# Squared-ReLU attention and a mixture of adapters: two stages through a transposed copy in DRAM, against one pipeline of 64x64 tiles

## The chip, the cores and the metric

One core of a Trainium2 chip runs the whole kernel as one launch. The metric is the device time of that core in microseconds, the median of repeated executions; lower is better.

## What is computed

For 8 batches of 12 heads, q, k and v are 448 x 64 each, in f32. The attention has no softmax; its output becomes 3584 rows of 768, on which each row picks the best two of eight adapters of rank 16:

```python
scores = scale * np.matmul(q, k.transpose(0, 1, 3, 2))
attn = np.maximum(scores, 0.0) ** 2 / S
attn_out = np.matmul(attn, v)
x = attn_out.transpose(0, 2, 1, 3).reshape(B * S, H * D)
logits = x @ w_gate
topk = np.argpartition(-logits, 2, axis=1)[:, :2]
...
delta[mask] += w[mask, k, None] * ((x[mask] @ A[e]) @ B[e])
return x + delta
```

The weights w are the softmax over the two chosen logits.

## The kernel before

The work has two stages that follow one another.

The attention stage goes over the 8 batches, and in each over 12 heads in two groups of six. `do_prepass` (L74 to L84) loads a group of q and of k as f32 on SP's queue, casts q on ScalarE (L81) and k on VectorE (L83) to bf16 and stores both into DRAM tensors `q_bf` and `k_bf`. `do_transpose` (L86 to L95) reads them back with a transposing DMA, so that `qT` and `kT` have the 64 values of a head on the partitions. v is loaded in four pieces a batch (L104) and cast in one instruction on ScalarE (L111).

For each head there are four chunks of up to 128 keys (128, 128, 128 and 64). A chunk is one score matmul (L125, 64 rows of the array, 128 or 64 columns, 448 queries streamed), one ReLU with scale (two heads of three on ScalarE, L137; every third on VectorE, L135), one square on VectorE (L138), and one value matmul (L139, 128 or 64 rows, 64 columns, 448 streamed) that accumulates `outT` over the chunks. A head's result is copied from PSUM into `xt` (L149 on VectorE, L151 on ScalarE), which holds x transposed for all 3584 rows.

The adapter stage goes over 7 chunks of 512 rows. It computes z (L184, all adapters at once as 128 columns), the logits of 128 rows at a time (L199), the routing weights in eight short instructions on VectorE and an exponential on ScalarE (L207 to L221), expands and transposes them (L226 to L230), multiplies (L233), applies B in f32 (L238), adds x (L245), transposes back in f32 (L250), copies (L256) and stores (L257).

The order of the instructions on each engine comes from the framework's own scheduling of the program; the pools' buffers (six for scores, two for outT) limit how far it runs ahead. The pools of the attention stage are closed before those of the adapter stage are opened.

Of the kernel before, what the change touches and what calls it, by code (L numbers as in the profile page):

```python
# [9 lines left out]
F32 = mybir.dt.float32  # L11
F32R = mybir.dt.float32
BF16 = mybir.dt.bfloat16


@with_exitstack
def kernel(
# [10 lines left out]
    nc = tc.nc  # L28
# [28 lines left out]
    k_bf = k_bf_flat[:TOT].rearrange("(b h s d) -> b h s d", b=B, h=H, s=S)

    TCH = (S + 127) // 128
    tsz = [min(128, S - i * 128) for i in range(TCH)]  # L60

    attn_ctx = ExitStack()
    attn_sbuf = attn_ctx.enter_context(tc.tile_pool(name="attn_sbuf", bufs=4))
    attn_psum = attn_ctx.enter_context(tc.tile_pool(name="attn_psum", bufs=2, space=bass.MemoryType.PSUM))
    vb_pool = attn_ctx.enter_context(tc.tile_pool(name="vb", bufs=2))
    pp_pool = attn_ctx.enter_context(tc.tile_pool(name="pp", bufs=2))

    zt = pp_pool.tile([128, 1], BF16, tag="zt", bufs=1)
    nc.vector.memset(zt, 0.0)
    nc.sync.dma_start(out=q_bf_flat[TOT:].rearrange("(p f) -> p f", p=128), in_=zt)  # L70
    nc.sync.dma_start(out=k_bf_flat[TOT:].rearrange("(p f) -> p f", p=128), in_=zt)

    qT_pool = attn_ctx.enter_context(tc.tile_pool(name="qT_pool", bufs=3))

    def do_prepass(b, g):
        for i, (src, dst) in enumerate(((qflat, qbf2), (kflat, kbf2))):
            tf = pp_pool.tile([128, PPC], F32, tag=f"tf{i}")
            nc.sync.dma_start(out=tf, in_=src[b, g])
            tb = pp_pool.tile([128, PPC], BF16, tag=f"tb{i}")
            if i == 0:  # L80
                nc.scalar.copy(tb, tf)  # L81
            else:
                nc.vector.tensor_copy(tb, tf)  # L83
            nc.sync.dma_start(out=dst[b, g], in_=tb)  # L84

    def do_transpose(b, g):  # L86
        qT = qT_pool.tile([128, HS, S], BF16, tag="qT")
        kT = qT_pool.tile([128, HS, S], BF16, tag="kT")
        q_src = bass.AP(tensor=q_bf.tensor, offset=(b * H + g * HS) * S * Dh,
                        ap=[[Dh, HS * S], [1, 2 * Dh]])  # L90
        k_src = bass.AP(tensor=k_bf.tensor, offset=(b * H + g * HS) * S * Dh,
                        ap=[[Dh, HS * S], [1, 2 * Dh]])
        nc.sync.dma_start(out=qT.rearrange("p h s -> p (h s)"), in_=q_src, transpose=True)  # L93
        nc.sync.dma_start(out=kT.rearrange("p h s -> p (h s)"), in_=k_src, transpose=True)
        return qT, kT  # L95

    bg_list = [(b, g) for b in range(B) for g in range(NSPLIT)]
    do_prepass(0, 0)
    qTkT = {(0, 0): None}
    for b in range(B):  # L100
        v_f = vb_pool.tile([128, TCH, H, Dh], F32, tag="v_f")
        for tc_i in range(TCH):
            ts = tsz[tc_i]
            nc.sync.dma_start(  # L104
                out=v_f[:ts, tc_i],
                in_=v[b, :, tc_i * 128 : tc_i * 128 + ts, :].transpose([1, 0, 2]),
            )
        if tsz[-1] < 128:
            nc.vector.memset(v_f[64:128, TCH - 1], 0.0)
        v_bf = vb_pool.tile([128, TCH, H, Dh], BF16, tag="v_bf")  # L110
        nc.scalar.copy(v_bf, v_f)  # L111

        for h in range(H):
            g = h // HS
            bg_idx = b * NSPLIT + g
            if h % HS == 0:
                if bg_idx + 1 < len(bg_list):
                    do_prepass(*bg_list[bg_idx + 1])
                qT, kT = do_transpose(b, g)
            hg = h - g * HS  # L120
            outT_ps = attn_psum.tile([64, S], F32, tag="outT", bufs=2)
            for tc_i in range(TCH):
                ts = tsz[tc_i]
                scores_ps = attn_psum.tile([128, 512], F32, tag="scores", bufs=6)
                nc.tensor.matmul(  # L125
                    out=scores_ps[:ts, :S],
                    lhsT=kT[:Dh, hg, tc_i * 128 : tc_i * 128 + ts],
                    rhs=qT[:Dh, hg, :],
                    start=True,
                    stop=True,  # L130
                )
# [6 lines left out]
                nc.vector.tensor_mul(attn2_bf[:ts], attn_bf[:ts], attn_bf[:ts])  # L138
                nc.tensor.matmul(  # L139
                    out=outT_ps,  # L140
                    lhsT=v_bf[:ts, tc_i, h, :],
                    rhs=attn2_bf[:ts],
                    start=(tc_i == 0),
                    stop=(tc_i == TCH - 1),
                )
            p0 = (h % 2) * 64
            dst = xt[p0 : p0 + 64, h // 2, b * S : b * S + S]
            if h % 2:
                nc.vector.tensor_copy(dst, outT_ps)  # L149
            else:  # L150
                nc.scalar.copy(dst, outT_ps)  # L151

    attn_ctx.close()

    wg_sb = const_pool.tile([128, DO, E], BF16)
    nc.gpsimd.dma_start(out=wg_sb, in_=moe_w_gate.rearrange("(do di) e -> di do e", di=128))

    A_sb = const_pool.tile([128, DO, E, R], BF16)
    for do in range(DO):
# [128 lines left out]
```

## Time and profile before

| | us |
|---|---|
| median of 3 runs | 541.85 |
| lowest and highest run | 539.98, 545.13 |
| the profiled execution: span from the first to the last instruction | 544.2 |
| TensorE matmul busy | 456.5 |
| VectorE busy | 337.3 |
| ScalarE busy | 199.8 |

The page gives the profiled execution by its span alone. It lies inside the runs. Busy time of TensorE's matmuls counts from a matmul's start to its modelled end, so two that follow closely overlap; the pitch between two starts is read from the timeline. A row of the timeline that merges n instructions gives the start of the first and the time to the end of the last.

### The profile page before, as it was taken

The numbers are of one execution on the slowest core, as the hardware profiler recorded it, in microseconds if no ns is written. First come the engines' busy times: TensorE is split into PE (matmuls) and PEld (weight loads), VectorE is DVE, ScalarE is ACT, GpSimd is POOL, SyncE is SP. The second block draws the span as 40 slices with busy tenths as digits, with TensorE's granted clock in tenths as the row PEclk, the third lists the DMA queues.
The fourth block names the chain that finished last, engine by engine and source line by source line (L and its number), as shares of the span: only waits on it lengthen the run. The fifth ranks groups of instructions, "written<-read, shape, count | busy, mean of one in ns | idle before, by whom it ended". The sixth has DMA issues, their size and how long they took to land.

```text
span 544.2 us, 4703 instructions
## 1 busy us (share of the span) xinstructions
PE 456.5 (84%) x1253; PEld 134.5 (25%) x1258; DVE 337.3 (62%) x921; ACT 199.8 (37%) x385; POOL 6.9 (1%) x13
## 2 busy tenths in 40 slices
PE   0004999999999999999999999999998798888874
PEld 0001222222221221222122222212222345454532
DVE  1003667566676756756665665766557779897863
ACT  1033374355337445535644554454333111111000
POOL 5000000000000000000000000000000000000000
PEclk9999999999999999999999999999999989896877
DMA  9979929907955981991597199046000013131222
GB/s 100 144 254 255 279 98 255 295 8 203 210 197 126 240 242 45 221 272 70 136 235 237 44 226 263 5 118 136 0 1 0 1 47 137 73 151 59 116 117 116
DMA packets 151292, 77.99 MB, mean 143 GB/s; under 512 B 139361, under 2 KB 139361, under 8 KB 151265
## 3 DMA queue, kind: packets, MB, share of 16 engines
q1 hardware_dynamic: 144240, 77.48, 55.9%
q0 software_dynamic: 7024, 0.21, 2.6%
q8 instruction: 10, 0.16, 0.1%
q14 instruction: 18, 0.14, 0.1%
HBM read 33.84 MB, written 22.02 MB: 103 GB/s over the span
## 4 chain that ended last, share of the span: by engine, by line
PE 76%; DVE 13%; DMA 6%; SPq 2%; issue 2%; ACT 0%; ACTq 0%
PE outT_ps L139 33%; PE scores_ps L125 30%; PE d_ps L238 8%; PE tr_ps L250 4%; DMA tf<-in_k_dram 3%; DVE out_nd L256 3%; DVE xt L149 3%; DVE attn_bf L138 3%; PE zT_ps L184 1%; DMA tf<-in_q_dram 1%; DVE sumT_sb L245 1%; SPq L104 1%; DMA kT<-k_bf 1%; SPq L93 1%; DVE wexpT_sb L230 1%
## 5 line engine op out<-in xcount | busy, mean ns | idle before, releaser
L125 PE MATMUL scores_ps<-qT,kT 64*128 64x448 bf16 (+1 forms) x384 | 191.7, 562 | 48.2 <-DMA kT<-k_bf 48.2
L139 PE MATMUL outT_ps<-attn_bf,v_bf 128*64 128x448 bf16 (+1 forms) x384 | 197.1, 577 | 13.7 <-DVE attn_bf L138 12.5
L138 DVE TENSOR_TENSOR attn_bf<-attn_bf 128x448 bf16<-128x448 bf16 (+1 forms) x384 | 132.9, 381 | 53.6 <-PE outT_ps L139 35.7
L137 ACT ACTIVATE attn_bf<-scores_ps 128x448 bf16<-128x448 f32 (+1 forms) x256 | 122.6, 539 | 100.5 <-DVE attn_bf L138 75.3
L125 PEld LDWEIGHTS <-kT 64*128 64x128 bf16 (+1 forms) x384 | 37.7, 112 | 201.2 <-issue 153.0
L149 DVE CAST xt<-outT_ps 64x448 bf16<-64x448 f32 x48 | 29.6, 618 | 82.5 <-PE outT_ps L139 82.5
L139 PEld LDWEIGHTS <-v_bf 128*64 128x64 bf16 (+1 forms) x384 | 44.4, 133 | 140.0 <-issue 125.7
L135 DVE TENSOR_SCALAR attn_bf<-scores_ps 128x448 bf16<-128x448 f32 (+1 forms) x128 | 74.2, 609 | 1.3 <-PE scores_ps L125 1.3
L151 ACT CAST xt<-outT_ps 64x448 bf16<-64x448 f32 x48 | 25.2, 525 | 101.4 <-PE outT_ps L139 101.4
L238 PE MATMUL d_ps<-zpT_sb,B_sb 128*128 128x512 f32 x84 | 50.4, 739 | 1.5 <-DVE zpT_sb L233 1.4
L250 PE MATMUL tr_ps<-ident,sumT_sb 128*128 128x128 f32 x168 | 30.2, 308 | 11.7 <-DVE out_nd L256 9.6
L83 DVE CAST tb<-tf 128x1344 bf16<-128x1344 f32 x16 | 13.6, 849 | 38.4 <-DMA tf<-in_k_dram 38.4
L245 DVE TENSOR_TENSOR sumT_sb<-d_ps,xt 128x512 f32<-128x512 f32 x42 | 28.8, 689 | 13.0 <-PE d_ps L238 12.8
L111 ACT CAST v_bf<-v_f 128x3072 bf16<-128x3072 f32 x8 | 22.0, 2748 | 26.8 <-DMA v_f<-in_v_dram 26.8
L256 DVE COPY out_nd<-tr_ps 128x768 f32<-128x768 f32 x28 | 26.7, 955 | 7.5 <-PE tr_ps L250 6.8
L250 PEld LDWEIGHTS tr_ps<-ident,sumT_sb 128*128 128x128 f32 x168 | 21.7, 155 | 24.1 <-DVE out_nd L256 14.5
L226 ACT COPY w_exp<-w_sb 128x128 f32<-128x128 f32 x28 | 8.3, 296 | 49.9 <-DVE w_sb L221 24.1
L238 PEld LDWEIGHTS d_ps<-zpT_sb,B_sb 128*128 128x128 f32 x84 | 17.7, 235 | 20.8 <-issue 8.4
L81 ACT CAST tb<-tf 128x1344 bf16<-128x1344 f32 x16 | 20.4, 1310 | 3.5 <-DMA tf<-in_q_dram 2.6
L213 ACT ACTIVATE w_sb<-sub 128x8 f32<-128x8 f32 x28 | 5.8, 208 | 38.9 <-DVE sub L211 30.6
L229 PE MATMUL wexp_ps<-ident,w_exp 128*128 128x128 f32 x28 | 9.4, 338 | 5.6 <-ACT w_exp L226 4.9
L184 PE MATMUL zT_ps<-xt,A_sb 128*128 128x512 bf16 x37 | 12.6, 439 | 1.1 <-DVE xt L149 0.8
(26 smaller groups left out, 98.9 us busy)
## 6 DMA issues: line engine op xcount, KB each, us to landing
tf<-in_q_dram SPq DMA_DIRECT2D x16, 672.0 KB, 6.6
tf<-in_k_dram SPq DMA_DIRECT2D x16, 672.0 KB, 7.6
out_dram<-out_nd SPq DMA_DIRECT2D x28, 384.0 KB, 2.3
v_f<-in_v_dram SPq DMA_DIRECT2D x24, 384.0 KB, 5.0
q_bf<-tb SPq DMA_DIRECT2D x16, 336.0 KB, 2.7
k_bf<-tb SPq DMA_DIRECT2D x16, 336.0 KB, 2.9
v_f<-in_v_dram SPq DMA_DIRECT2D x8, 192.0 KB, 5.6
B_sb<-in_moe_B_dram SPq DMA_DIRECT2D x1, 384.0 KB, 7.5
```

The costliest lines, as they stand in the source:

```text
L111: nc.scalar.copy(v_bf, v_f)
L125: nc.tensor.matmul(out=scores_ps[:ts, :S], lhsT=kT[:Dh, hg, tc_i * 128 : tc_i * 128 + ts], rhs=qT[:Dh, hg, :], start=True, stop=True,)
L135: nc.vector.tensor_scalar(attn_bf[:ts], scores_ps[:ts, :S], relu_scale, 0.0, op0=mybir.AluOpType.mult, op1=mybir.AluOpType.max)
L137: nc.scalar.activation(attn_bf[:ts], scores_ps[:ts, :S], mybir.ActivationFunctionType.Relu, scale=relu_scale)
L138: nc.vector.tensor_mul(attn2_bf[:ts], attn_bf[:ts], attn_bf[:ts])
L139: nc.tensor.matmul(out=outT_ps, lhsT=v_bf[:ts, tc_i, h, :], rhs=attn2_bf[:ts], start=(tc_i == 0), stop=(tc_i == TCH - 1),)
L149: nc.vector.tensor_copy(dst, outT_ps)
L151: nc.scalar.copy(dst, outT_ps)
L238: nc.tensor.matmul(out=d_ps[:, :ncur], lhsT=B_sb[:, do * 128 : do * 128 + 128], rhs=zpT_sb[:, :ncur], start=True, stop=True,)
L245: nc.vector.tensor_add(sumT_sb[:, do, :ncur], d_ps[:, :ncur], xt_c[:, do, :])
L250: nc.tensor.transpose(tr_ps[:ns, do * 128 : do * 128 + 128], sumT_sb[:, do, j * 128 : j * 128 + ns], ident,)
L256: nc.vector.tensor_copy(out_nd[:ns], tr_ps[:ns])
```

## The change

The new kernel keeps what is computed and changes how all of it is laid out and ordered. The 448 positions of a head are taken as 64 partitions times 7 (J), so that a position is 7 p + j. Batches are loaded by POOL with a cast from f32 to bf16 in the DMA, six heads on the lower 64 partitions and six on the upper. A quad is four heads: two slots (sl) times two halves (g, or a on the key side). Two jobs of 14 transposes on TensorE per quad make qT and kT. A step is one j of a quad: four score matmuls, one ReLU, one square, and, two steps later (LAG), four value matmuls, each of 64x64 on its own quarter of the array. The adapter work is written as a generator of short pieces, `job_moe`; one piece runs between the score and the value matmuls of those steps of a quad that don't transpose (j of 0, 2, 4, 5, 6). The order is written out by hand (`manual_schedule`).

The core of the diff, where line numbers of the new kernel in the text below (L112 and so on) are those of its file:

```diff
-    const_pool = ctx.enter_context(tc.tile_pool(name="const", bufs=1))
-    q_bf_flat = nc.dram_tensor("q_bf", (TOT + PAD,), BF16)
-    k_bf_flat = nc.dram_tensor("k_bf", (TOT + PAD,), BF16)
...
-    def do_prepass(b, g):
-    def do_transpose(b, g):
...
+    loads = ctx.enter_context(tc.tile_pool(name="loads", bufs=3))
+    apool = ctx.enter_context(tc.tile_pool(name="apool", bufs=4))
+    ps_s = ctx.enter_context(tc.tile_pool(name="ps_s", bufs=2, space=bass.MemoryType.PSUM))
+    ps_o = ctx.enter_context(tc.tile_pool(name="ps_o", bufs=1, space=bass.MemoryType.PSUM))
+    ps_m = ctx.enter_context(tc.tile_pool(name="ps_m", bufs=2, space=bass.MemoryType.PSUM))
+    ctx.enter_context(tc.manual_schedule())
...
+    def load_batch(b, per_quad=False):
...
+        parts = [(2 * c, 2 * c + 2) for c in range(NC_)] if per_quad else [(0, HH)]
+        for s0, s1 in parts:
+            for t, src in zip(tiles, (qv, kv, vv)):
+                for g in range(2):
+                    nc.gpsimd.dma_start(
+                        out=t[g * PH : g * PH + PH, s0:s1, :], in_=src[b, g, :, s0:s1, :]
+                    )
...
+    def job_transpose(qi, which):
...
+        for j in range(J):
+            for sl in range(2):
+                nc.tensor.transpose(
+                    ps[sl * PH : sl * PH + PH, j * 128 : j * 128 + 128],
+                    src[:, 2 * c + sl, j * Dh : j * Dh + Dh],
+                    identb,
+                )
+        yield
...
+        nc.vector.tensor_copy(sb.rearrange("p j a s -> p (j a s)"), ps)
...
+    def job_moe(bp, tiles_):
...
+                nc.tensor.matmul(
+                    out=z[:, t * ZW : t * ZW + ZW],
+                    lhsT=xt[:, do, c0[t] : c0[t] + 128],
+                    rhs=awg[:, do, :],
...
+        yield
...
+        nc.scalar.activation(w[:, :T], sub[:, :T], ACTF.Exp)
...
+        yield
...
+                    nc.tensor.matmul(
+                        out=o[:, i * 128 : i * 128 + 128],
+                        lhsT=xt[:, d0 + i, c0[t] : c0[t] + 128],
+                        rhs=identb,
...
+                nc.tensor.matmul(
+                    out=o[:, : nd * 128],
+                    lhsT=zT[:, t * 128 : t * 128 + 128],
+                    rhs=B_sb[:, d0 * 128 : (d0 + nd) * 128],
...
+    def emit_qk(n):
...
+        for sl in range(2):
+            r0 = sl * PH
+            for a in range(2):
+                nc.tensor.matmul(
+                    out=s[a * PH : a * PH + PH, sl, 0:S].rearrange("p (j s) -> p j s", j=J),
+                    lhsT=kT[r0 : r0 + PH, j, a, :],
+                    rhs=qT[r0 : r0 + PH, :, a, :],
...
+    def emit_relu(n):
+        a1 = apool.tile([128, 2, S], BF16, name=f"a1_{n}", tag="a1")
+        nc.scalar.activation(a1, sc[n][:, :, 0:S], ACTF.Relu, scale=relu_scale)
+        a2 = apool.tile([128, 2, S], BF16, name=f"a2_{n}", tag="a2")
+        nc.vector.tensor_mul(a2, a1, a1)
...
+    def emit_pv(n):
...
+        for g in range(2):
+            r0 = g * PH
+            for sl in range(2):
+                nc.tensor.matmul(
+                    out=oT[qi][g][sl * PH : sl * PH + PH, 0:S],
+                    lhsT=vn[r0 : r0 + PH, 2 * c + sl, j * Dh : j * Dh + Dh],
+                    rhs=at2[n][r0 : r0 + PH, sl, :],
...
+    def emit_xt(qi):
+        b, c = quads[qi]
+        nc.scalar.copy(xt[:, c, b * S : b * S + S], oT[qi][0][:, 0:S])
+        nc.vector.tensor_copy(xt[:, NC_ + c, b * S : b * S + S], oT[qi][1][:, 0:S])
...
+    for n in range(total + LAG + 1):
+        qi, j = divmod(n, J)
+
+        m = n - LAG - 1
+        if m >= 0 and m % J == J - 1:
+            emit_xt(m // J)
...
+        if n < total:
...
+            emit_qk(n)
+
+        if n < total and qi + 1 < NQ and j in (1, 3):
+            active.append(job_transpose(qi + 1, 0 if j == 1 else 1))
...
+        if n < total and j in (1, 3) and qi + 1 < NQ:
+            pass
+        elif todo:
+            try:
+                next(todo[0])
+            except StopIteration:
+                todo.pop(0)
+        if n < total:
+            emit_relu(n)
+        if 0 <= n - LAG < total:
+            emit_pv(n - LAG)
+    for g in todo:
+        run(g)
```

Three places show what moves in the order of an engine's instructions.

The first is TensorE where the adapter products stand. Before, the end of the attention stage: the last value matmuls (L139, into outT_ps) and then the first adapter products (L184, into zT_ps).

```order
L139 LDWEIGHTS v_bf
L139 MATMUL outT_ps<-attn_bf,v_bf 64x448
L184 LDWEIGHTS A_sb
L184 MATMUL zT_ps<-xt,A_sb 128x512
L184 LDWEIGHTS A_sb
```

After, in the middle of the attention: the last pieces of one adapter output (o, L189 and L197), the four value matmuls of a step (L252, into the two outT tiles), and the first score matmul of the next step (L228).

```order
L189 MATMUL o_0_2_899<-identb,xt 128x128
L197 MATMUL o_0_2_899<-B_sb,zT_0_737 128x512
L252 LDWEIGHTS vn_118
L252 MATMUL oT_4_795<-a_33_866,vn_118 64x448
L252 LDWEIGHTS vn_118
L252 MATMUL oT_4_795<-a_33_866,vn_118 64x448
L252 LDWEIGHTS vn_118
L252 MATMUL oT_4_796<-a_33_866,vn_118 64x448
L252 LDWEIGHTS vn_118
L252 MATMUL oT_4_796<-a_33_866,vn_118 64x448
L228 LDWEIGHTS kT_834
L228 MATMUL s_913<-qT_782,kT_834 64x448
```

The adapter products moved from behind all attention into the queue between a step's score matmuls and the value matmuls of two steps before.

The second place is the transposing of q and k. Before, it is on SP's queue: loads (L78), stores of the bf16 copy (L84) and transposing loads (L93, L94).

```order
L78 DMA tf<-in_q_dram 128x1344
L84 DMA q_bf<-tb 128x1344
L84 DMA k_bf<-tb 128x1344
L78 DMA tf<-in_k_dram 128x1344
L93 DMA_TRANSPOSE qT<-q_bf 128x2688
L94 DMA_TRANSPOSE kT<-k_bf 128x2688
```

After, it is on TensorE, directly behind a step's score matmuls (L228); 14 such transposes (L112) of qn, the loaded q, follow one another.

```order
L228 LDWEIGHTS kT_834
L228 MATMUL s_913<-qT_782,kT_834 64x448
L112 LDWEIGHTS qn_166
L112 MATMUL tp_6_918<-identb,qn_166 64x128
L112 LDWEIGHTS qn_166
L112 MATMUL tp_6_918<-identb,qn_166 64x128
```

What was a DMA on a queue of its own is now ahead of the value matmuls and of the next step's scores in TensorE's queue.

The third place is ScalarE in the attention. Before, ReLUs (L137), the copies of the result (L151) and the cast of v (L111).

```order
L151 CAST xt<-outT_ps 64x448
L137 ACTIVATE attn_bf<-scores_ps 128x448 x3
L137 ACTIVATE attn_bf<-scores_ps 64x448
L151 CAST xt<-outT_ps 64x448
L137 ACTIVATE attn_bf<-scores_ps 128x448 x2
L111 CAST v_bf<-v_f 128x3072
```

After, the ReLUs of steps 23 to 28 (L238), with the exponential of a routing job (L151) and the copy of its transposed product (L180) between them.

```order
L238 ACTIVATE a_23_630<-s_604 128x896
L238 ACTIVATE a_24_660<-s_640 128x896
L151 ACTIVATE w_0_681<-sub_0_679 128x24
L238 ACTIVATE a_25_685<-s_668 128x896
L238 ACTIVATE a_26_707<-s_693 128x896
L238 ACTIVATE a_27_724<-s_715 128x896
L180 COPY zT_0_737<-zt_0_720 128x384
L238 ACTIVATE a_28_739<-s_732 128x896
```

The ReLU is twice as wide and all on ScalarE; the casts are gone, and adapter instructions stand ahead of ReLUs.

## Rows read from the trace of the kernel before

**Rows 1.** The page: busy us, and the span in 40 slices.

```profile
PE 456.5 (84%) x1253; PEld 134.5 (25%) x1258; DVE 337.3 (62%) x921; ACT 199.8 (37%) x385; POOL 6.9 (1%) x13
...
PE   0004999999999999999999999999998798888874
...
PEclk9999999999999999999999999999999989896877
```

**Rows 2.** Busy time by stage: stretch, its length, engines, granted clock, DMA, GB/s.

```profile
core 0: us, PE busy (x) PEld busy (x) DVE busy (x) ACT busy (x) POOL busy (x), PEclk, DMA share, GB/s
0.00:48.20 48.20, 0.00 (x0) 0.00 (x0) 4.74 (x7) 7.87 (x5) 6.92 (x13) 1.00 1.17 182
48.20:425.00 376.80, 362.07 (x773) 81.18 (x775) 239.63 (x578) 178.83 (x324) 0.00 (x0) 1.00 0.62 154
425.00:544.20 119.20, 94.44 (x482) 53.33 (x484) 92.97 (x336) 13.13 (x56) 0.00 (x0) 0.82 0.24 93
```

**Rows 3.** The chain that ended last, its start: start us, us, what.

```profile
2.14 18.31 DMA tf<-in_k_dram
...
43.29 4.89 DMA kT<-k_bf
...
48.23 1.81 PE scores_ps L125 x4
```

**Rows 4.** Timeline of TensorE near 200 us: start, us, what, count.

```profile
200.84 0.58 PE L125 MATMUL scores_ps<-qT,kT 64*64 64x448 bf16 x1
201.21 0.58 PE L139 MATMUL outT_ps<-attn_bf,v_bf 64*64 64x448 bf16 x1
...
202.20 0.96 PE L139 MATMUL outT_ps<-attn_bf,v_bf 128*64 128x448 bf16 x2
...
203.46 0.55 PE L125 MATMUL scores_ps<-qT,kT 64*128 64x448 bf16 x1
203.94 0.58 PE L139 MATMUL outT_ps<-attn_bf,v_bf 64*64 64x448 bf16 x1
```

**Rows 5.** The adapter stage: timeline rows of TensorE, one group of VectorE.

```profile
443.54 0.38 PE L250 MATMUL tr_ps<-ident,sumT_sb 128*128 128x128 f32 x2
443.75 0.27 PE L229 MATMUL wexp_ps<-ident,w_exp 128*128 128x128 f32 x1
...
444.43 0.38 PE L184 MATMUL zT_ps<-xt,A_sb 128*128 128x512 bf16 x1
...
445.13 0.59 PE L184 MATMUL zT_ps<-xt,A_sb 128*128 128x512 bf16 x2
...
441.52 1.96 PE L238 MATMUL d_ps<-zpT_sb,B_sb 128*128 128x512 f32 x4
...
L216 DVE TENSOR_TENSOR w_sb<-w_sb,mask 128x8 f32<-128x8 f32 x28 | 4.4, 159 | 0.2
```

**Rows 6.** POOL's DMA issues; DMAs by line: KB each, median us to landing.

```profile
L160 POOL DMA_DIRECT2D A_sb<-in_moe_A_dram x6 | 5.3, 908 | 0.0
...
tf<-in_q_dram SPq DMA_DIRECT2D x16, 672.0 KB, 6.6
...
out_dram<-out_nd SPq DMA_DIRECT2D x28, 384.0 KB, 2.3
```

**Rows 7.** ScalarE and VectorE: groups (busy, mean ns), two timeline rows.

```profile
L137 ACT ACTIVATE attn_bf<-scores_ps 128x448 bf16<-128x448 f32 x192 | 94.1, 540 | 89.4 <-DVE attn_bf L138 65.7 <-PE scores_ps L125 23.6
...
L149 DVE CAST xt<-outT_ps 64x448 bf16<-64x448 f32 x48 | 29.6, 618 | 82.5 <-PE outT_ps L139 82.5
...
L111 ACT CAST v_bf<-v_f 128x3072 bf16<-128x3072 f32 x8 | 22.0, 2748 | 26.8 <-DMA v_f<-in_v_dram 26.8
L81 ACT CAST tb<-tf 128x1344 bf16<-128x1344 f32 x16 | 20.4, 1310 | 3.5 <-DMA tf<-in_q_dram 2.6 <-ACT tb L81 0.9
...
202.25 1.83 ACT L137 ACTIVATE attn_bf<-scores_ps 128x448 bf16<-128x448 f32 x4
...
199.75 1.29 DVE L138 TENSOR_TENSOR attn_bf<-attn_bf 64x448 bf16<-64x448 bf16 x4
```

More of the change, by code (lines that the diff above doesn't have):

```diff
@@ L57 @@
[L57 to L66, printed above, removed]
@@ new lines @@
+    ps_m = ctx.enter_context(tc.tile_pool(name="ps_m", bufs=2, space=bass.MemoryType.PSUM))
+    xt = const.tile([128, DO, N], BF16)
+    awg = const.tile([128, DO, ZW], BF16)
+    B_sb = const.tile([128, D], F32)
+    identf = const.tile([128, 128], F32)
+    identb = const.tile([128, 128], BF16)
+    ctx.enter_context(tc.manual_schedule())
+    qv, kv, vv = (
+        t.rearrange("b (g s) (p j) d -> b g p s (j d)", g=2, j=J) for t in (q, k, v)
+    )
+    batches = {}
+    def load_batch(b, per_quad=False):
+        tiles = [
+            loads.tile([128, HH, J * Dh], BF16, name=f"{nm}n{b}", tag=f"{nm}n") for nm in "qkv"
+        ]
+        batches[b] = tiles
+        parts = [(2 * c, 2 * c + 2) for c in range(NC_)] if per_quad else [(0, HH)]
[5 more added lines that the diff above has]
+                    )
@@ new lines @@
+    make_identity(nc, identf)
+    nc.vector.tensor_copy(identb, identf)
+    load_batch(0, per_quad=True)
+    nc.sync.dma_start(out=B_sb, in_=moe_B.rearrange("e r d -> (e r) d"))
+    load_batch(1)
+    nc.gpsimd.dma_start(
+        out=awg[:, :, RE:ZW], in_=moe_w_gate.rearrange("(do di) e -> di do e", di=128)
+    )
+    for do in range(DO):
+        nc.gpsimd.dma_start(
+            out=awg[:, do, 0:RE].rearrange("p (e r) -> p e r", e=E),
+            in_=moe_A[:, do * 128 : do * 128 + 128, :].transpose([1, 0, 2]),
+        )
@@ new lines, with misc @@
+    quads = [(b, c) for b in range(B) for c in range(NC_)]
+    NQ = len(quads)
+    qkT = {}
+    def misc(name):
+        return ps_m.tile([128, 512], F32, name=name, tag="misc")
+    def job_transpose(qi, which):
+        b, c = quads[qi]
+        src = batches[b][which]
+        ps = ps_m.tile([128, J * 128], BF16, name=f"tp{which}_{qi}", tag="misc")
+        for j in range(J):
[4 more added lines that the diff above has]
+                    identb,
+                )
+        yield
+        sb = tpool.tile([128, J, 2, PH], BF16, name=f"{'qk'[which]}T{qi}", tag=f"{'qk'[which]}T")
+        nc.vector.tensor_copy(sb.rearrange("p j a s -> p (j a s)"), ps)
+        qkT[qi, which] = sb
@@ L138 @@
[L138 to L159, printed above, removed]
-        nc.gpsimd.dma_start(out=A_sb[:, do], in_=moe_A[:, do * 128 : do * 128 + 128, :].transpose([1, 0, 2]))
-    A_flat = A_sb.rearrange("p do e r -> p do (e r)")
-    B_sb = const_pool.tile([128, D], F32R)
-    nc.sync.dma_start(out=B_sb, in_=moe_B.rearrange("e r d -> (e r) d"))
@@ new lines, in emit_relu @@
+    def emit_relu(n):
[3 more added lines that the diff above has]
+        nc.vector.tensor_mul(a2, a1, a1)
+        at2[n] = a2
+    def emit_pv(n):
+        qi, j = divmod(n, J)
+        b, c = quads[qi]
+        vn = batches[b][2]
+        if j == 0:
+            oT[qi] = [ps_o.tile([128, 512], F32, name=f"oT{g}_{qi}", tag=f"oT{g}") for g in range(2)]
+        for g in range(2):
[5 more added lines that the diff above has]
+                    rhs=at2[n][r0 : r0 + PH, sl, :],
+                    start=(j == 0),
+                    stop=(j == J - 1),
+                )
```

275 lines of the change are left out of this document (120 added, 155 removed).

## The prediction

> **What bounds the kernel now.** I read first the page's busy times and the slices of the span, then the busy times by stage, then the chain at the start, then the single matmuls of the middle stage. The slices show three stages: none of TensorE's work at first, a long stretch at 9 tenths, and a last part whose granted clock falls [rows 1]. By stage [rows 2]: 48.2 us in which TensorE does nothing, 376.8 us of attention in which it is busy for 362.1 us at the full clock (1.00, the 2.4 GHz level), and 119.2 us of adapters, where it is busy for 94.4 us and the granted clock is 0.82 on average. So the span is start + TensorE's attention + adapters, one after the other.
>
> The start is a chain of loads: the first k tile takes 18.31 us, and after a trip through DRAM and back the last link, the transposing load of kT, ends at 48.2 us, where the first matmul stands [rows 3].
>
> In the attention stage 768 matmuls take 362 us, 0.47 us each. The reader should see why [rows 4]: two matmuls of one shape start 0.96 - 0.58 = 0.38 us apart; in the shape that the change uses throughout, 64x64, 201.21 - 200.84 = 0.37 us; and where the shape changes, 203.94 - 203.46 = 0.48 us. A 512-column matmul on the whole array starts 0.59 - 0.38 = 0.21 us after the one before [rows 5], so 448 columns are worth about 0.19 us; the rest, 0.18 us, is the weight load and a gap that nothing hides, plus about 0.12 us at a change of shape.
>
> **The change part by part.**
>
> *Start.* Gone are the store and reload through DRAM, the casts of q, k and v on ScalarE and VectorE, and the DMA transposes. POOL now issues the loads, 0.91 us an issue [rows 6]; the identity matrix stands ahead of them. Two issues for q and two for k are out by about 5.5 us; a load of the old tile lands 6.6 us after its issue at the median, and these are a third of its size, so I take 3.5 us: 9 us. Then 28 transposes, two copies out of PSUM and one semaphore trip, 6 us. First scores at about **15 us**; 10 to 30 are the bounds, 30 if the first quad waits as the old k tile did.
>
> *Loads later on.* 33 MB of f32 come in 18,432 runs of 1792 bytes. One tile after the other at 688 KB in 6.6 us, they would take 317 us; the old kernel moved 182 GB/s in its first stage [rows 2], which makes it 181 us. Both are under the sum below, so I cost it at nothing; the cover is the work of two batches, since three buffers let a batch load while the two ahead of it are used. No row shows a casting load of this size.
>
> *Attention steps.* There are 24 quads of 7 steps, 168 steps, each with four score matmuls and four value matmuls of 64x64. The trace never shows two tiles of the array at work together. From below: one tile's own pitch, 0.37 us for a group of four. From above: four in single file, 4 x 0.37 = 1.48 us. I take 0.40, near the lower end, since the four differ in rows or in columns of the array and each has 0.18 us of weight load and gap in which the others could stream. So 0.80 us for TensorE per step. ScalarE's ReLU now covers 896 columns in one instruction: 448 take 0.540 us alone, and four back to back start (1.83 - 0.54) / 3 = 0.43 us apart; of the casts from SBUF, a further column costs (2748 - 1310) / (3072 - 1344) = 0.83 ns [rows 7], so 448 more add 0.37: 0.80 to 0.91, I take 0.86. Four of VectorE's squares take 1.29, 0.32 each, so one of twice the width takes at most 0.65 us. ScalarE sets the pace: 168 x 0.86 = **145 us**. What is late next behind the old matmul stall is thus the ReLU, by a thin margin.
>
> *The transposes* are new on TensorE: 48 jobs of 14, on all 128 rows and alternately in two column halves. One half's chain is 0.19 us beyond the columns (0.38 - 0.19) plus 128 columns at 0.42 ns, 0.24 us. Singly that is 0.24 a piece, with both halves overlapping 0.12; a bare stream of 128 columns would be 0.054. I take 0.12, as for the four tiles. Two changes of shape add about 0.13 each. 14 x 0.12 + 0.27 less the 0.06 that TensorE is ahead of ScalarE: 1.88 a job, **90 us** (47 to 170). They are on the path: there are two score buffers, the next scores and the value matmuls are queued behind the transposes, and ScalarE waits for those scores. VectorE's copy of 896 columns is at most twice the 0.618 of L149 [rows 7], beside TensorE's work.
>
> *The adapters* move between the steps. Per 128 rows: six logit-and-z matmuls of 136 columns and six identity ones of 128 (0.42 ns a column: 0.67 us), an f32 transpose (0.38 - 0.27 = 0.11 us) and the f32 product of 512 + 256 columns. Four f32 passes of 512 columns take 1.96 us with the tail of the last [rows 5], 0.43 us a pass, so two passes over 768 columns are 1.29. Together 2.07 us. Of 28 tiles the loop takes 23 outputs and 24 first products, 48 us; its 66 visits each cost two changes of shape less ScalarE's slack, 0.21: **62 us**. These also stand ahead of the value matmuls in TensorE's queue.
>
> *New waits.* In each routing job the exponential stands ahead of a ReLU in ScalarE's queue and waits for VectorE's square (0.65) and four short instructions of 0.16 [rows 5]: 1.3 us. In its next visit TensorE's transposes wait for a further 1.4 us of VectorE's work, of which half shows. 10 jobs in the loop x 2.0 = **20 us**. Once a quad, ScalarE's copy of the attention result (448 columns, 0.54) stands ahead of a ReLU: 24 x 0.54 = **13 us**.
>
> *Tail.* The old 119.2 us shrink to what follows the last step: five output tiles and two routing jobs of two tiles, in series. About 1.6 us for the first output, 8 us for each job (1 us of products, 3 us of short instructions with their trips, 3.2 us of outputs) and 2.3 us for the last store to land [rows 6], **21 us** (15 to 35, if the clock falls as in the old last stage).
>
> Sum: 15 + 145 + 90 + 62 + 20 + 13 + 21 = **366 us** of span. The profiled span of 544.2 lies 0.4% above the median of the runs, 541.85; the page gives nothing around it, so I scale by that: **364 us**.
>
> VectorE's own load is some 9 us a quad (7 squares at 0.65, two copies at 1.2 at most, one at 0.62, the routing) against 14 us for a quad, and has cover; without that cover its 24 x 9 = 216 us would be a floor.
>
> A rule speaks against the column halves. The Trainium skill, "TensorE: Matmul & The Clock Gate", Part 3, What overlaps and what doesn't, says that a weight load overlaps matmuls in flight only when its row group differs. No run here shows it, as before has one tile alone; by that rule the sum would be the first rival's, by mine 366.
>
> **Rivals.**
>
> 1. *The two column halves of one set of rows work in file* (slower). Place: TensorE's queue, where the second tile of each pair has the same rows as the first. Then a group of four costs 2 x 0.37 = 0.74, a step 1.48 and a job of transposes 14 x 0.24 = 3.36: 15 + 168 x 1.48 + 48 x (3.36 + 0.27) + 66 x 0.27 + 48 + 20 + 13 + 21 = 558, scaled **556 us**. For it: the unhidden 0.18 us behind every small matmul shows that a load can wait for the matmul before it. Against: the pairs that wait there are one and the same tile. It decides where the groups and transposes together pass 544 - 148 = 396 us; the 148 being all the other terms with the changes of shape; the forecast has 225 there (145 + 80), this rival 410 (249 + 161). This is the case that the rule of the Trainium skill above would make.
> 2. *The tiles do not overlap at all*, so the change does not do what it says: 8 x 0.37 = 2.96 a step, 497 + 174 + 66 + 69 = 806, scaled **803 us**. For it: nothing in the trace shows an overlap. Against: the whole array hides its loads [rows 5], so TensorE does load beside a stream.
> 3. *The loads set the pace*: one tile landing after another, 2 + 317 us, then the last batch's three quads (44) and the tail, 384, scaled **382 us**. For it: the median landing. Against: stretches of the start at 182 GB/s.
>
> **How the numbers follow.** Forecast 0.74, with its own range 290 to 445: below with bare-stream transposes (-43), half of the waits and a short tail (-30), above with single transposes (+80). Rival 1 has 0.12, rival 2 0.05, rival 3 0.09. The range of all is 290 to 510: it holds the forecast, rival 3 and partial overlap on the way to rival 1, and leaves out about 2 in 10. Within 1% is about what three runs spread over 5 us can tell. Faster by more: 0.74 + 0.09 and a sixth of rival 1, 0.85; within 1%: 0.02 from rival 1; slower 0.13.
>
> **What would show it.** Right: first score matmul near 15 us; plain steps 0.86 us apart with ScalarE near 9 tenths; four score matmuls starting within 0.1 us of each other and the next four 0.40 later; a transposing step of 2.7 us; about 21 us after the last value matmul. Wrong: starts 0.37 us apart inside a group (rivals 1 and 2); transposes 0.24 apart; a step that waits for a load (rival 3); a granted clock under 1.00 in the middle, which no term allows for.

## The result, and the profile after

The kernel after takes 275.88 us (median of four runs, 274.34 to 279.84); the kernel before, run beside it, 543.49 us (539.98 to 545.66). The ratio is 0.507, with a 95% interval of 0.503 to 0.511. The direction was forecast; the size was not: 364 us was predicted, and the time lies below the low end of the range, 290. Of the experiments below, `e1` and `e4` are told by their faster execution, the profiled one, since the other took longer (507.55 and 398.73 us), and `e5` by its fastest, since its other three took longer.

The page of the profiled execution, first the lines that answer to [rows 1], then the chain of waits by engine and by line:

```profile
span 273.5 us, 6096 instructions
...
PE 205.1 (75%) x2492; PEld 100.3 (37%) x2492; DVE 169.2 (62%) x397; ACT 177.7 (65%) x245; POOL 45.2 (17%) x73
...
PE   0877759976795997898697687788686866789762
...
PEclk9999997999999599599999999799959979979799
...
PE 44%; DVE 21%; ACT 19%; issue 8%; POOL 4%; DMA 2%; ACTq 0%; POOLq 0%
```

No engine fills the span: TensorE, VectorE and ScalarE take turns on the chain. The granted clock is uneven, 0.93 on average, and its dips stand in the middle too, where no term of the prediction allowed for them.

The busy time by stage (length; busy us and instructions of each engine; granted clock; DMA share; GB/s), with cuts at the first ReLU, at the end of the three quads that run without adapter work, and at the last ReLU, as [rows 2] had it for before:

```profile
0.00:9.94 9.94, 2.56 (x36) 1.68 (x36) 1.47 (x3) 1.29 (x2) 9.12 (x20) 1.00 0.88 145
9.94:30.64 20.70, 16.11 (x244) 8.10 (x241) 16.37 (x28) 18.44 (x23) 14.13 (x20) 1.00 2.21 162
30.64:246.40 215.76, 169.19 (x2115) 81.33 (x2114) 144.00 (x338) 151.84 (x210) 21.90 (x34) 0.92 0.53 97
246.40:273.50 27.10, 17.22 (x104) 9.22 (x102) 7.40 (x29) 6.13 (x13) 0.00 (x0) 0.93 0.39 102
```

The start is 9.9 us, a quad without adapter work 6.9 us (20.70 / 3), the rest of the loop 215.8 us, the tail 27.1 us. Against [rows 2] the start lost 38 us; attention and adapters, 376.8 + 119.2 = 496 us one after the other, now take 263.6 us together.

TensorE's timeline in the middle answers to [rows 4]. A row gives the start of the first instruction, the time to the end of the last, and their count:

```profile
101.49 0.38 PE L252 MATMUL oT<-a,vn 64*64 64x448 bf16 x4
101.70 0.36 PE L228 MATMUL s<-qT,kT 64*64 64x448 bf16 x4
101.89 0.36 PE L252 MATMUL oT<-a,vn 64*64 64x448 bf16 x4
102.08 0.36 PE L228 MATMUL s<-qT,kT 64*64 64x448 bf16 x4
102.37 0.58 PE L112 MATMUL tp<-identb,qn 128*64 128x128 bf16 x14
102.88 0.38 PE L252 MATMUL oT<-a,vn 64*64 64x448 bf16 x4
```

Four matmuls together take no longer than one: the rows of four are 0.36 to 0.38 us long, and the next four start 0.19 to 0.21 us later. A whole job of 14 transposes stands between 102.08 and 102.88: 0.80 us with the group of four ahead of it. The same shapes at the very start of the same kernel look different:

```profile
6.40 0.96 PE L112 MATMUL tp<-identb,qn 128*64 128x128 bf16 x14 [6.40 <-DMA qn<-in_q_dram]
...
9.30 0.96 PE L228 MATMUL s<-qT,kT 64*64 64x448 bf16 x8 [0.72 <-DVE kT L119]
```

Here 14 transposes take 0.96 us instead of 0.58, and two groups of four 0.96 us. The trace holds the clock as a list of entries, each with its start, its length and its level (1.0 or 0.5), and the first entry begins at 13.74 us; so at 9.30 the granted clock is printed without having been recorded. This contrast led to the experiments. The same test, made on before, on the adapter products that it runs both ahead of and behind the first entry of its own clock record (426.95 us):

```profile
423.62 1.91 PE L184 MATMUL zT_ps<-xt,A_sb 128*128 128x512 bf16 x4 [0.22 <-issue]
...
427.44 0.59 PE L184 MATMUL zT_ps<-xt,A_sb 128*128 128x512 bf16 x2
...
423.62 0.63 PE L184 MATMUL zT_ps<-xt,A_sb 128*128 128x512 bf16 x1 [0.22 <-issue]
...
423.00:426.90 3.90, 3.68 (x15) 1.51 (x15) 1.21 (x5) 0.00 (x0) 0.00 (x0) 1.00 0.01 2
426.95:428.00 1.05, 1.05 (x16) 0.57 (x14) 0.42 (x5) 0.21 (x1) 0.00 (x0) 1.00 0.00 0
```

At 423.62 the starts lie (1.91 - 0.63) / 3 = 0.427 us apart, which is 512 columns at 1.2 GHz; at 427.44 the pair is 0.59 us long with one at 0.38 [rows 5], 0.21 us apart, which is 512 columns at 2.4 GHz. Yet the clock is printed as 1.00 in both stretches. So the 1.00 of [rows 2] over before's attention stands for "no record", not for the full clock.

### The profile page after: what moved, and what is told of

The parts are those of the page before. It is cut to its first block, busy times and chain, and to the rows that moved or that the text cites. A ratio compares the mean times of both kernels' runs of the same rounds, so it can differ in the third digit from the quotient of the medians.

```text
span 273.5 us, 6096 instructions
## 1 busy us (share of the span) xinstructions
PE 205.1 (75%) x2492; PEld 100.3 (37%) x2492; DVE 169.2 (62%) x397; ACT 177.7 (65%) x245; POOL 45.2 (17%) x73
## 4 chain that ended last, share of the span: by engine, by line
PE 44%; DVE 21%; ACT 19%; issue 8%; POOL 4%; DMA 2%; ACTq 0%; POOLq 0%
ACT a L238 15%; PE o L197 15%; PE oT L252 10%; DVE a L240 9%; PE s L228 7%; PE o L189 6%; ACT o L208 3%; DVE kT L119 3%; DMA qn<-in_q_dram 2%; DVE xt L263 2%; PE tp L112 2%; PE zt L175 2%; DVE zp L166 2%; POOL qn L80 2%; PE z L133 2%
## 5 line engine op out<-in xcount | busy, mean ns | idle before, releaser
L238 ACT ACTIVATE a<-s 128x896 bf16<-128x896 f32 x168 | 148.6, 921 | 43.9 <-PE s L228 42.9
L240 DVE TENSOR_TENSOR a<-a 128x896 bf16<-128x896 bf16 x168 | 103.5, 623 | 76.0 <-ACT a L238 74.7
L252 PE MATMUL oT<-a,vn 64*64 64x448 bf16 x672 | 71.6, 390 | 13.5 <-DVE a L240 4.8
L228 PE MATMUL s<-qT,kT 64*64 64x448 bf16 x672 | 68.0, 381 | 10.9 <-ACT a L238 10.2
L197 PE MATMUL o<-B_sb,zT 128*128 128x512 f32 (+1 forms) x112 | 53.0, 559 | 0.5 <-ACT zT L180 0.5
L252 PEld LDWEIGHTS <-vn 64*64 64x64 bf16 x672 | 23.5, 108 | 61.2 <-issue 49.8
L228 PEld LDWEIGHTS <-kT 64*64 64x64 bf16 x672 | 24.3, 112 | 18.9 <-issue 14.9
L189 PE MATMUL o<-identb,xt 128*128 128x128 bf16 x168 | 20.5, 236 | 12.0 <-ACT o L208 8.3
L208 ACT COPY o<-o 128x512 f32<-128x512 f32 x28 | 16.5, 589 | 16.6 <-PE o L197 16.6
L189 PEld LDWEIGHTS <-xt 128*128 128x128 bf16 x168 | 12.3, 104 | 34.3 <-issue 29.5
L112 PE MATMUL tp<-identb,qn 128*64 128x128 bf16 x336 | 15.8, 241 | 6.6 <-DMA qn<-in_q_dram 6.6
L197 PEld LDWEIGHTS o<-B_sb,zT 128*128 128x128 f32 x112 | 18.8, 210 | 0.8 <-ACT zT L180 0.8
L119 DVE COPY qT<-tp 128x896 bf16<-128x896 bf16 x24 | 14.8, 615 | 5.8 <-PE tp L112 5.8
L210 DVE COPY o<-o 128x256 f32<-128x256 f32 x28 | 11.7, 418 | 10.6 <-PE o L197 10.6
L112 PEld LDWEIGHTS <-qn 128*64 128x64 bf16 x336 | 11.6, 121 | 15.7 <-issue 8.4
L112 PE MATMUL tp<-identb,kn 128*64 128x128 bf16 x336 | 15.1, 233 | 0.3 <-DMA kn<-in_k_dram 0.3
L119 DVE COPY kT<-tp 128x896 bf16<-128x896 bf16 x24 | 14.8, 618 | 0.6 <-PE tp L112 0.6
```

Of the source, the lines that this page charges most:

```text
L112: nc.tensor.transpose(ps[sl * PH : sl * PH + PH, j * 128 : j * 128 + 128], src[:, 2 * c + sl, j * Dh : j * Dh + Dh], identb,)
L119: nc.vector.tensor_copy(sb.rearrange("p j a s -> p (j a s)"), ps)
L189: nc.tensor.matmul(out=o[:, i * 128 : i * 128 + 128], lhsT=xt[:, d0 + i, c0[t] : c0[t] + 128], rhs=identb, start=(i == 0), stop=False, ski ...
L197: nc.tensor.matmul(out=o[:, : nd * 128], lhsT=zT[:, t * 128 : t * 128 + 128], rhs=B_sb[:, d0 * 128 : (d0 + nd) * 128], start=False, stop=True,
L208: nc.scalar.copy(dst, o[:, : nd * 128])
L228: nc.tensor.matmul(out=s[a * PH : a * PH + PH, sl, 0:S].rearrange("p (j s) -> p j s", j=J), lhsT=kT[r0 : r0 + PH, j, a, :], rhs=qT[r0 : r0 ...
```

## The experiments

**Theory A**: the attention stage of before ran at the 1.2 GHz level, and its 0.37 us per small matmul is 448 columns at that level (0.373) with the weight load hidden. **Theory B**: the prediction's reading, 0.19 us of stream and 0.18 us of a weight load and a gap that one tile can't hide, and which the four tiles cover for each other.

**One tile for everything** (`e1`, from the kernel after; the ReLU, the square and the copies are narrowed to the same 64 partitions):

```diff
-                    out=s[a * PH : a * PH + PH, sl, 0:S].rearrange("p (j s) -> p j s", j=J),
-                    lhsT=kT[r0 : r0 + PH, j, a, :],
-                    rhs=qT[r0 : r0 + PH, :, a, :],
+                    out=s[0:PH, sl, 0:S].rearrange("p (j s) -> p j s", j=J),
+                    lhsT=kT[0:PH, j, a, :],
+                    rhs=qT[0:PH, :, a, :],
...
-                    out=oT[qi][g][sl * PH : sl * PH + PH, 0:S],
-                    lhsT=vn[r0 : r0 + PH, 2 * c + sl, j * Dh : j * Dh + Dh],
-                    rhs=at2[n][r0 : r0 + PH, sl, :],
+                    out=oT[qi][g][0:PH, 0:S],
+                    lhsT=vn[0:PH, 2 * c + sl, j * Dh : j * Dh + Dh],
+                    rhs=at2[n][0:PH, sl, :],
```

> The new kernel with all eight matmuls of a step put on one and the same 64x64 tile of the array (rows and columns 0 to 63), so the other halves of the result are left at zero. Theory A (weight loads are hidden; the 0.37 us pitch of the old kernel was 448 columns at the 1.2 GHz level, in a stretch for which the profile has no clock record): eight starts 0.19 us apart at 2.4 GHz, a step of at least 1.5 us and about 400 us in all; or, if TensorE falls to the low level with so little of the array in use, 0.37 us apart, 3.0 us a step and about 650 us, and then the 136-column adapter matmuls beside them go at 0.11 instead of 0.06 us. Theory B (the prediction's: 0.18 us of weight load and gap stand bare behind every matmul of one tile, at any clock): 0.37 us apart with the adapter matmuls still at 0.06, about 650 us. Rival, overlap of tiles is worth nothing because ScalarE sets the pace: 276 us.

Measured: 428.95 us. TensorE's timeline, ahead of and behind the first entry of the run's clock record, which is at 91.9 us:

```profile
60.75 1.70 PE L229 MATMUL s<-qT,kT 64*64 64x448 bf16 x4
...
150.47 0.92 PE L229 MATMUL s<-qT,kT 64*64 64x448 bf16 x4
```

With one matmul of 0.58 and 0.35 us, the starts lie (1.70 - 0.58) / 3 = 0.37 and (0.92 - 0.35) / 3 = 0.19 us apart. One instruction, one tile, a new weight load each time, and two pitches in the ratio of the two clock levels: 0.19 us is the bare stream of 448 columns at 2.4 GHz, so nothing of the load shows. Theory B has no way to 0.19 on a single tile; it falls. The run also prices the overlap of the four tiles: 428.95 against 275.88, about 150 us in this execution, the stretch at the low level ahead of 91.9 us included.

**Value matmuls of before on all columns** (`e2`), **score matmuls on all rows** (`e9`), **both** (`e3`), each from the kernel before:

```diff
-            outT_ps = attn_psum.tile([64, S], F32, tag="outT", bufs=2)
+            outT_ps = attn_psum.tile([128, S], F32, tag="outT", bufs=2)
...
-                    lhsT=v_bf[:ts, tc_i, h, :],
+                    lhsT=v_bf[:ts, tc_i, h - h % 2 : h - h % 2 + 2, :].rearrange("p a d -> p (a d)"),
```

```diff
-                    lhsT=kT[:Dh, hg, tc_i * 128 : tc_i * 128 + ts],
-                    rhs=qT[:Dh, hg, :],
+                    lhsT=kT[:, hg, tc_i * 128 : tc_i * 128 + ts],
+                    rhs=qT[:, hg, :],
```

> The kernel before with one edit: each value matmul takes the columns of two heads (128 instead of 64) and the copy keeps the half that belongs to its head; the count of matmuls and their 448 streamed columns are as before. Theory A: if the granted clock rises with that, value matmuls start 0.19 to 0.22 us apart instead of 0.37, TensorE is no longer the bound of the attention stage, and the total falls to about 450 to 490 us; if it does not rise, 542 us. Theory B: the loads stay bare, 0.37 us apart, 540 us or a little more.

> As the run with wide value matmuls, and the score matmuls take all 128 partitions of kT and qT as well (the second 64 hold the neighbouring position's values, so the scores are other numbers). Every full chunk now uses the whole array with the same streamed columns. Theory A: the granted clock rises to 2.4 GHz in the attention stage, pitches of 0.19 to 0.22 us, 430 to 480 us in all. Theory B: 0.34 to 0.38 us between starts as before, about 540 us.

> The kernel before with the score matmuls alone on all 128 rows of the array (both operands taken over 128 partitions instead of 64, so a score also sums over 64 further rows and its values are others); the value matmuls stay 64 columns wide. Theory A1 (the rows of the score matmuls are what the level hangs on): the clock record starts early, starts of single matmuls lie near 0.19 us instead of 0.35 to 0.37, and the time is near that of the run with both parts, 440 to 455 us. Theory A2 (both the rows of the scores and the columns of the value matmuls are needed): starts stay near 0.35 to 0.37 us apart in the attention and the time stays at 535 to 545 us.

Measured: 537.24 us with wide value matmuls, ratio to before 0.987 (0.975 to 1.000); 449.85 us with wide scores, 0.829 (0.816 to 0.842); 442.09 us with both, 0.812 (0.805 to 0.820). The timelines near 200 us, of `e2`, of `e9` and of `e3`:

```profile
202.83 0.55 PE L139 MATMUL outT_ps<-attn_bf,v_bf 64*128 64x448 bf16 x1
203.18 0.58 PE L125 MATMUL scores_ps<-qT,kT 64*128 64x448 bf16 x1
```

```profile
213.80 0.35 PE L139 MATMUL outT_ps<-attn_bf,v_bf 128*64 128x448 bf16 x1
213.99 0.35 PE L125 MATMUL scores_ps<-qT,kT 128*64 128x448 bf16 x1
```

```profile
199.79 0.35 PE L139 MATMUL outT_ps<-attn_bf,v_bf 128*128 128x448 bf16 x1
199.98 0.35 PE L125 MATMUL scores_ps<-qT,kT 128*128 128x448 bf16 x1
```

In `e2` the starts stay 0.35 us apart and its clock record begins only at 425.7 us; in the others they come down to 0.19, and the record begins at 58.3 and 56.3 us, a few us into the attention. (0.35 is a little under the 0.373 of 448 columns at 1.2 GHz. In before's attention too only 64x64 neighbours start 0.37 apart throughout, two of one wider shape 0.32 to 0.37; no run here explains that.) The number of matmuls and their 448 streamed columns are the same in all three. So about 100 us of before's time was its clock level (543.49 - 442.09), and wide score matmuls alone bring 94 of them, as theory A1 had it. That it is no more than 100 fits VectorE as the next bound, which was not tested; the stages of `e3`:

```profile
51.70:323.00 271.30, 221.14 (x767) 68.67 (x767) 238.78 (x577) 176.22 (x324) 0.00 (x0) 0.95 0.88 214
```

VectorE is busy for 239 of 271 us there, against 240 of 377 before [rows 2]. These runs don't show what sets the level in general: `e1`, with 64 rows in every score and value matmul, is at the full level without a break from 91.9 to 409 us.

**Both column halves of one set of rows** (`e4`, from the kernel after), the case of rival 1:

```diff
-            r0 = sl * PH
+            r0 = 0
...
-            r0 = g * PH
+            r0 = 0
```

> The new kernel with every score and value matmul on the array's rows 0 to 63, so that a group of four uses two column halves of one set of rows instead of four quarters; the results of the second set of rows are replaced. Theory A: the two columns of a pair start 3 ns apart and a group takes 2 x 0.19 = 0.37 us, a step 0.75, still under ScalarE's 0.80: about 285 us (276 to 310). The prediction's first rival (column halves of one set of rows in file): 0.19 or 0.37 us between any two starts, a step of 1.5 to 3.0 us, 400 us or more.

Measured: 383.76 us, far from the 285 us that Theory A gave. TensorE's timeline at full clock and in a stretch at 0.5, and the stages:

```profile
82.70 0.56 PE L252 MATMUL oT<-a,vn 64*64 64x448 bf16 x4
83.10 0.54 PE L228 MATMUL s<-qT,kT 64*64 64x448 bf16 x4
83.48 0.54 PE L252 MATMUL oT<-a,vn 64*64 64x448 bf16 x4
...
110.10 0.95 PE L252 MATMUL oT<-a,vn 64*64 64x448 bf16 x4
110.85 0.95 PE L228 MATMUL s<-qT,kT 64*64 64x448 bf16 x4
...
9.00:68.70 59.70, 58.98 (x390) 28.68 (x389) 29.02 (x57) 30.94 (x37) 22.85 (x33) 1.00 1.26 134
68.70:96.00 27.30, 23.96 (x251) 12.17 (x250) 15.85 (x36) 18.39 (x24) 2.63 (x4) 1.00 0.61 111
96.00:382.00 286.00, 264.22 (x1825) 121.85 (x1825) 126.33 (x303) 134.78 (x183) 11.82 (x18) 0.69 0.28 57
```

Groups of four start 0.38 to 0.40 us apart at full clock: two pairs in file, each pair in the time of one matmul, its two starts 3 ns apart. Had the halves worked in file it would be 4 x 0.19 = 0.76. So column halves of the same rows do overlap. What missed was the time. The clock record begins only at 68.7 us, and ahead of it pairs start 0.37 us apart, so the 1.00 of the first stage is again no record; from 96 us on the granted clock is 0.69, and groups stretch to 0.75 us where it is 0.5. Nothing in Theory A foresaw so much of the low level. What separates this run's clock from that of the kernel after (0.92 there, with the same instructions on twice the rows) was not tried further.

**No interleaving** (`e5`): all adapter work behind the attention.

```diff
-        elif todo:
+        elif False:
```

> The new kernel with no adapter piece between the attention steps: all twelve routing jobs run behind the last value matmul. Theory A (attention alone is paced by ScalarE: the three quads of the new kernel without adapter work take 6.7 to 7.0 us each): start 10 + 24 x 7.0 + adapters in series at about 4.8 us per 128 rows, as in the new kernel's tail, 28 x 4.3 to 4.8 = 120 to 135: about 300 to 310 us, so the interleaving is worth some 30 us. By the prediction's terms: 364 less the adapters' 62 and 20 in the loop, plus 23/5 of the tail's 21: about 380 us. Rival, the adapters are free in the loop: 24 x 7 + 10 + 24 would have been 202 for the new kernel, which it is not.

Measured: 299.68 us in the fastest of four executions (up to 305.12); the profiled one, 305.12, has a granted clock of 0.83 in the adapters. Interleaving is worth some 24 us (299.68 - 275.88). The run shows bare attention: ScalarE's timeline of one quad, then two rows of TensorE's.

```profile
119.60 4.16 ACT L238 ACTIVATE a<-s 128x896 bf16<-128x896 f32 x5
123.60 0.58 ACT L262 CAST xt<-oT 128x448 bf16<-128x448 f32 x1
124.01 0.99 ACT L238 ACTIVATE a<-s 128x896 bf16<-128x896 f32 x1
125.60 2.75 ACT L238 ACTIVATE a<-s 128x896 bf16<-128x896 f32 x3 [0.60 <-PE s L228]
...
124.23 0.38 PE L252 MATMUL oT<-a,vn 64*64 64x448 bf16 x2 [0.61 <-ACT xt L262]
125.00 0.38 PE L252 MATMUL oT<-a,vn 64*64 64x448 bf16 x2 [0.39 <-DVE xt L263]
```

Five ReLUs in 4.16 us with one at 0.92 are (4.16 - 0.92) / 4 = 0.81 us apart, back to back. The copy of the result (0.41 from its start to the next ReLU's) and one wait of 0.60 are what mainly interrupts them, and the quads from the second on are 7.03 us each. The wait is not for transposes: the value matmuls of the new quad wait for the two copies of the old result, on ScalarE and on VectorE, since each of the two outT tiles has one buffer, and the next scores stand behind them in TensorE's queue. From the ReLU at 124.01 to the next are 1.59 us, 0.78 more than the pace.

**No transposes in the loop** (`e6`): the jobs after the first quad are left out, and all quads use the first quad's qT and kT.

```diff
+        qkT[qi, 0], qkT[qi, 1] = qkT[0, 0], qkT[0, 1]
...
-        if n < total and qi + 1 < NQ and j in (1, 3):
+        if False:
```

> The new kernel with the transposes of the first quad alone; every later quad uses that quad's qT and kT again, so the scores of the other quads are replaced by the first's; the 46 other jobs of 14 transposes and their copies are left out, the loads stay. The prediction's term (1.88 us a job on the path): 46 x 1.88 = 86 us less, about 190 us. Theory A (two column halves run together at 53 ns a pair, so a job holds TensorE for about 0.8 us, most of it beside the 0.80 us ReLU): 10 to 25 us less, 250 to 265 us. Rival, wholly hidden: 276 us.

Measured: 258.51 us, ratio to before 0.475 (0.472 to 0.477). The 46 jobs are worth 275.88 - 258.51 = 17.4 us, 0.38 us each. The prediction had 1.88 us each. The granted clock from 9.9 to 246 us is lower in `e6` than in the kernel after (0.86 against 0.93), so at one clock they may be worth somewhat more. A quad without adapter work, on ScalarE:

```profile
20.08 4.97 ACT L238 ACTIVATE a<-s 128x896 bf16<-128x896 f32 x6 [0.60 <-PE s L228]
...
26.89 4.36 ACT L238 ACTIVATE a<-s 128x896 bf16<-128x896 f32 x5 [0.60 <-PE s L228]
```

The wait of 0.60 stays without the transposes, and the quad takes 6.81 us instead of 7.03: there a job costs 0.11 us, so most of the 17.4 us arises beside adapter work.

**The adapter product in bf16** (`e7`), B loaded by POOL with a cast and zT written as bf16; then, on top of it, **the exponential one piece later** (`e8`), so that it no longer stands in ScalarE's queue while VectorE is still at its input:

```diff
-    B_sb = const.tile([128, D], F32)
+    B_sb = const.tile([128, D], BF16)
...
-        zT = mpool.tile([128, 3 * 128], F32, name=f"zT{bp}_{tiles_[0]}", tag="zT")
+        zT = mpool.tile([128, 3 * 128], BF16, name=f"zT{bp}_{tiles_[0]}", tag="zT")
```

```diff
-        nc.scalar.activation(w[:, :T], sub[:, :T], ACTF.Exp)
...
         yield
...
+        nc.scalar.activation(w[:, :T], sub[:, :T], ACTF.Exp)
```

> The new kernel with B and the transposed routed product in bf16, so the adapters' last product is one pass at 0.21 us per 512 columns instead of two at 0.49 (B comes by POOL with a cast). If TensorE sets the pace of the steps that hold such a product: 56 products cost about 0.8 and 0.4 us less each, 33 us of TensorE, of which 20 to 28 show: 248 to 256 us. If ScalarE does (ReLU 0.80 plus the 0.59 copy in the same step): 5 to 12 us less, 264 to 271 us. Rival, off the path: 276 us.

> As the run with B in bf16, and the exponential of a routing job moved to the start of the next piece, so that it no longer stands ahead of a ReLU while VectorE still works on its input. If that wait is on the path (17.5 us of ScalarE waiting for sub in twelve jobs of the new kernel, ten of them in the loop): 8 to 15 us less than the run with B in bf16. If ScalarE's lost time there is made up within the next steps: within 3 us of it.

Measured: 251.32 us, ratio to before 0.461 (0.459 to 0.464), and 239.66 us, 0.437 (0.433 to 0.441). So one bf16 pass in place of two f32 passes is worth 24.6 us, some 4 of them in the tail (23.0 us from the last ReLU instead of 27.1), and the exponential's place in the queue 11.7 us. ScalarE's waits in the kernel after, in `e7` and in `e8` (engine, line, what it waited for: total us, times, longest):

```profile
ACT a L238 <- PE s L228: 42.9, 53, 7.9
ACT w L151 <- DVE sub L147: 17.5, 12, 1.7
ACT o L208 <- PE o L197: 16.6, 15, 2.3
```

```profile
ACT a L238 <- PE s L228: 25.9, 37, 7.7
ACT w L151 <- DVE sub L147: 18.4, 12, 2.1
...
ACT o L208 <- PE o L197: 3.3, 4, 1.1
```

```profile
ACT a L238 <- PE s L228: 30.0, 40, 8.2
...
ACT w L156 <- DVE sub L147: 6.1, 6, 2.1
```

Each edit takes away the wait that it aims at: the ReLU's and the output copy's wait for TensorE lose 17.0 and 13.3 us in `e7`, the exponential's own 12.3 in `e8`, where 4.1 of the ReLU's wait come back. This last kernel is faster than the kernels before and after.

## Why the prediction was wrong

The sum against the measured stages, in us of span:

| term | predicted | measured | from |
|---|---|---|---|
| start | 15 | 9.9 | stages |
| attention steps, transposes, copies of x | 145 + 90 + 13 = 248 | 168 | 24 x 7.0, the bare quads of `e5` |
| adapters in the loop, routing waits | 62 + 20 = 82 | 68.5 | 246.4 - 9.9 - 168 |
| tail | 21 | 27.1 | stages |
| sum | 366 | 273.5 | |

The adapters' 68.5 is a remainder: it also holds what the transposes cost beside adapter work and what the lower clock cost.

**The step that failed** is one sentence of the first part: that 448 columns are worth 0.19 us and "the rest, 0.18 us, is the weight load and a gap that nothing hides". It set a duration from the adapter stage, whose clock was on record, against one from the attention, where none was, and took the printed 1.00 there as measured. The rows held the contradiction: a 64x64 matmul of 448 columns lasts 0.58 us in [rows 4], one of 512 columns on the whole array 0.38 us in [rows 5]. Fewer columns that last longer at the same clock ask for a reason, and `e1` names it: twice the clock, half the pitch.

**The transposes** carry most of the error, 90 us against about 17. The term put the supposed 0.19 us beyond the columns into every transpose, 0.24 us singly and 0.12 halved. Measured, the chain of 14 is 0.58 us long with a single one at about 0.24 (L112's mean): (0.58 - 0.24) / 13 = 0.026 each, two halves at once in the 0.053 of a bare stream. Even the bound from below, 47 us, still carried the change of shape at before's price and left TensorE 0.06 us a step ahead of ScalarE; with TensorE at 0.4 us a step, half of ScalarE's 0.81, most of a job falls into time that TensorE had free, as the 0.11 us a job of `e6`'s bare quad shows. A transposing step of 2.7 us was forecast; the steps of the bare quads take 0.8 to 1.6.

**The attention step** was right in its mechanism and its pace: ScalarE's ReLU sets it, 0.81 us instead of 0.86, that is 136 us instead of 145, and ScalarE is busy for 18.44 of 20.70 us in the quads without adapter work (151.84 of 215.76 beside it). That TensorE was ahead "by a thin margin" was not so: its 0.80 a step was twice the measured 0.40. The forecast of four starts within 0.1 us came true, the next four 0.40 later did not: 0.19 to 0.21. The copies of x, 13 us in the prediction, cost 24 x (0.41 + 0.78) = 29: it had ScalarE's copy ahead of a ReLU, but not the wait of the next quad's value matmuls for both copies.

**Adapters and routing** came out 13 us below their 82. They are on the path as forecast: the f32 product against one in bf16 (24.6 us by `e7`, some 20 of them in the loop) and the exponential (11.7 us by `e8`) make up nearly half of the 68.5. The exponential's own wait, forecast at 1.3 us for each job, is 17.5 / 12 = 1.46 us.

**The tail** was too small by 6 us counted from the last ReLU, by 3 counted from the end of the last value matmuls (249.93 us): the two last routing jobs begin their products at 251.85 and 260.92, 9.1 us apart instead of 8. **The start** was too large by 5: the first transposes stand at 6.40 us instead of 9, although the quad-sized loads land 4.5 us after their issue instead of 3.5, and from there to the first scores are 2.9 us (9.30 - 6.40) instead of 6.

**The rivals.** Rival 1 (column halves in file, 556 us) falls with `e4`: the pairs overlap. The rule of the Trainium skill, "TensorE: Matmul & The Clock Gate", Part 3, What overlaps and what doesn't, that a weight load overlaps matmuls in flight only when its row group differs, is not borne out here: in `e4` all rows are the same and a pair takes the time of one, and in `e1` even one tile hides its loads at 0.19 us a matmul. Rival 2 (no overlap, 803 us) falls with the timeline of after; it also carried the 0.37. Rival 3 (loads, 382 us) falls too: TensorE's waits for loads are 6.6 us in the transposes of q, of which 6.40 are the start, as the timeline above and their group show:

```profile
L112 PE MATMUL tp<-identb,qn 128*64 128x128 bf16 x336 | 15.8, 241 | 6.6 <-DMA qn<-in_q_dram 6.6
```

Forecast and rivals 1 and 2 were priced with the same 0.37, so the range could not reach low enough: its low end did take bare-stream transposes, which is what came, but at 47 us, nearly all of it on the path, where 17 are measured.

**The clock in the middle** fell below 1.00, as the last sentence on what would speak against the forecast had it. A product pair at the low level takes about twice its time (2.02 us at 243.80, granted clock 0.5, against 1.08 at 247.53), so the dips can only have lengthened TensorE's work and don't explain a time below the range:

```profile
243.80 2.02 PE L197 MATMUL o<-B_sb,zT 128*128 128x512 f32 x2
...
247.53 1.08 PE L197 MATMUL o<-B_sb,zT 128*128 128x512 f32 x2
```

## What to carry to other kernels

Before taking a clock from a profile, check it by the pitch of one instruction shape in two stretches: a printed 1.00 in a stretch without a clock record says nothing, and a shorter matmul that lasts longer gives the level away. Then price new work on TensorE by its streamed columns at the level it will get, with both levels as the bounds, before blaming loads that nothing hides. Where several engines share the path, ask of each instruction in an in-order queue whether its input is ready: moving one exponential by one piece was worth 12 us.

## What was not expected of the hardware

- Before's attention ran for 377 us with TensorE busy for 96% of it and its 64x64 matmuls at the pitch of 1.2 GHz; the same matmul count with scores on 128 rows instead of 64 reached the pitch of 2.4 GHz from 58 us on (granted clock 0.91 to 0.94), while widening the value matmuls alone did not (`e2`, `e9`). Yet `e1` held the full level for 317 us with every score and value matmul on one 64x64 tile.
- Four 64x64 tiles start about 3 ns apart and take the time of one; two column halves of the same rows do as well (`e4`), and a single tile hides its weight loads (`e1`).
- A copy of 896 bf16 columns out of PSUM takes VectorE 0.615 us (L119), hardly other than the 0.618 of 448 f32 columns [rows 7]: half of what the prediction bounded it by.
